# The pool engine gathers the second expert's rows ahead of all list scatters, and gets small copies that wait for the vector engine

## The chip, the cores and the metric

The kernel runs on one core of a Trainium2 chip. The metric is the device time in microseconds (us) of one execution; the number that counts is the median of several unprofiled runs. One further execution was taken with the hardware profiler, and all rows below are from it. PE is the matrix engine (PEld its weight loads), DVE the vector engine, ACT the scalar engine, POOL the engine that also issues indirect DMAs, SP the engine that issues most plain DMAs.

## The reference, cut to what matters

Three layers run one after the other: causal attention with a cumulative bias, a mixture of eight experts of which each token takes two, and a dense layer with the mish function. The change lies in the second:

```python
noisy_logits = x @ w_gate + np.log1p(np.exp(x @ w_noise)) * noise
top2 = np.argpartition(-noisy_logits, 2, axis=1)[:, :2]
top2_w = softmax over the two chosen logits
for e in range(8):
    for k in range(2):
        mask = top2[:, k] == e
        h = np.maximum(x[mask] @ w1[e], 0.0)
        out[mask] += top2_w[mask, k, None] * (h @ w2[e])
```

There are 1152 tokens of width 512; each expert has 1024 hidden units.

## The kernel before, in words

All of the work is issued in an order that is written out by hand, and each engine executes its own stream in that order. After attention the kernel routes: DVE picks the two experts of each token and works out a slot for each token in each expert's list, of 320 places (`CAP`). The lists of experts 0 and 1 are made at once on the chip (`quick_list`, line 737). The lists of all others are made in memory: 18 indirect DMAs from POOL (`scatter`, line 861) write token number and weight into the tensor `lst`, one DMA for 128 tokens and one of their two experts. Each later list comes back by three small loads from SP (`list_load`, line 767). With a list, three indirect DMAs from POOL fetch the rows of an expert's tokens into the tile `xg` (`xgather_chunk`, line 758).

An expert e is an up stage of eight steps f, some 1.8 us of PE each (line 897), and a down stage (line 962). After an up step ACT takes the positive part into the tile `HB[f]` (lines 899 and 900), and DVE writes what the rounding to the matrix format left out into the second part of the same tile (line 901). Then the step's hook `hup(f)` issues the side work of that step. In the down stage six hooks `hdn(c)` do the same; there the rows of expert e + 1 are also turned by PE (line 782) and split by ACT and DVE into `XH` and `XL` (lines 411 and 412). For experts 1 and 7 (`single`) the down stage goes through the eight `HB[f]` for the first block of rows before the second; for the others it goes through all three blocks for each f.

Side work is above all the preparing of weights for later: `convert` (line 254) has ACT copy a 128x512 weight to a rounded one (line 259) and either POOL or DVE subtract the two (line 260), which frees the raw tile for the next load from SP (lines 213 and 219). `narrow` (line 224) is DVE work alone, on integers, in three instructions for a weight of the third layer (lines 235, 237 and 239). Which engine subtracts stands in `MIXU` for the up steps (DVE for expert 0, POOL for all others) and in `MIXD` for the down stage (DVE and POOL by turns).

Before the change three scatters and the three gathers of expert 1 alternate ahead of the up stage of expert 0. Then each of its eight up hooks issues one scatter and a tiny POOL memset, and the down hooks call `scatter` twice each, until all 18 are out; that is in the seventh of these calls. A memset follows there in the calls in which POOL has no subtraction.

Of the kernel before, what the change touches and what calls it, by code (L numbers as in the profile page):

```python
# [9 lines left out]
F32 = mybir.dt.float32  # L10
# [18 lines left out]
CAP = 320  # L29
# [69 lines left out]
def f32(ap):  # L99
    return ap.bitcast(F32)  # L100
# [3 lines left out]
def kernel(ctx: ExitStack, tc: tile.TileContext, qT, kT, vv, ss, wg, nz, w1, w2,  # L104
# [55 lines left out]
    V, A, G_ = nc.vector, nc.scalar, nc.gpsimd  # L160
# [93 lines left out]
    def convert(sub, spare=0):  # L254

        for i, t in enumerate(tasks):
            if t["at"] == 5 and t["from"] <= at["now"] and t["step"] < at["step"] and len(places) > (spare if t["w"][0] >= 64 else 0):
                w = held[t["w"]] = places.pop(0)
                A.activation(w[:, 0], t["sv"], AF.Copy)  # L259
                sub(w[:, 1], t["sv"], f32(w[:, 0]))  # L260
                del tasks[i]
                if t["last"]:
                    at["out"] -= 1
                    fetch()
                return

    def work(subs, nv=0, spare=0):

        at["step"] += 1
        for i in range(max(len(subs), nv)):  # L270
            if i < len(subs):
                convert(subs[i], spare)
            if i < nv:
                narrow()
        start()
# [134 lines left out]
    def split(src, dsth, dstl):  # L410
        A.activation(dsth, src, AF.Copy)  # L411
        V.tensor_sub(dstl, src, f32(dsth))
# [99 lines left out]
    with tc.manual_schedule():  # L512
# [118 lines left out]
        for it in range(H + 2):  # L631
# [12 lines left out]
            for name in ORDERS[min(it, 3) if it < H - 1 else it - H + 5]:  # L644
                i = it + ("," not in name) + ("'" in name) - 1
# [6 lines left out]
    keep = ctx.enter_context(tc.tile_pool(name="keep", bufs=1, reuse_waits="tile"))  # L652
# [98 lines left out]
    XG, XH, XL = {}, {}, {}  # L751

    def xgather(e, idx):
        XG[e] = mp1.tile([128, 3, 512], F32, name="xg")
        for j in range(3):
            xgather_chunk(e, idx, j)

    def xgather_chunk(e, idx, j):
        m = BLK[j]
        nc.gpsimd.indirect_dma_start(  # L760
            out=XG[e][0:m, j], out_offset=None, in_=xd[:, :],
            in_offset=bass.IndirectOffsetOnAxis(ap=idx[0:m, j, 0:1], axis=0))
# [4 lines left out]
    def list_load(e, name="list"):  # L767
        idx = mp2.tile([128, 3, 2], I32, name=name, bufs=4 if name == "list" else None)
        r0 = first_row(e)
        nc.sync.dma_start(idx[:, 0:2], lst[r0:r0 + 256, :].rearrange("(j p) o -> p j o", p=128))  # L770
        for i in range(2):
            nc.sync.dma_start(idx[BLK[2] * i:BLK[2] * i + BLK[2], 2], lst[r0 + 256:r0 + CAP, :])
        return idx

    def xprep(e, c):
        if c == 0:
            XH[e] = mp1.tile([128, 4, CAP], F32R, name="xh")
            XL[e] = mp1.tile([128, 4, CAP], F32R, name="xl")
        xg = XG[e]
        t = next(psR)  # L780
        for j, m in enumerate(BLK):
            nc.tensor.transpose(t[:, 128 * j:128 * j + m], xg[0:m, j, 128 * c:128 * c + 128], identf[0:m, 0:m])  # L782
        split(t[:, :CAP], XH[e][:, c], XL[e][:, c])
# [77 lines left out]
    def scatter():  # L861


        if len(scat) < 2 * NT:
            t = len(scat) // 2
            ix = (idxa, idxb)[len(scat) % 2]
            st_ = nc.gpsimd.indirect_dma_start(
                out=lst[:, :], out_offset=bass.IndirectOffsetOnAxis(ap=ix[:, t:t + 1], axis=0),
                in_=tokw[:, t, len(scat) % 2], in_offset=None)
            for o in scat:  # L870
                tc.declare_no_dep(st_.ins, o.ins, reason="every slot is written once")
            scat.append(st_)

    for _ in range(2):
        convert(G_.tensor_sub)
    XG[1] = mp1.tile([128, 3, 512], F32, name="xg")
    for j in range(3):
        scatter()
        xgather_chunk(1, idx1, j)

    V.tensor_tensor(bcmp, inb[0:1, None, :].to_broadcast([1, NOV, E]),
# [7 lines left out]
    def up(e, hook):  # L889
        for f in range(8):  # L890
            ws = weight(8 * e + f // 2, f % 2)
            ps = next(psU)
            n = 0
            for c in range(4):
                wh, wl = ws[:, 0, 128 * c:128 * c + 128], ws[:, 1, 128 * c:128 * c + 128]
                for lhs, rhs in ((wh, XH[e][:, c]), (wh, XL[e][:, c]), (wl, XH[e][:, c])):
                    nc.tensor.matmul(ps[:, :CAP], lhs, rhs, start=n == 0, stop=n == 11)  # L897
                    n += 1
            nc.scalar.activation(HB[f][:, :CAP], ps[:, :CAP], AF.Relu)
            nc.scalar.activation(HB[f][:, 2 * CAP:], ps[:, 256:CAP], AF.Relu)  # L900
            V.scalar_tensor_tensor(HB[f][:, CAP:2 * CAP], ps[:, :CAP], 0.0, f32(HB[f][:, :CAP]),  # L901
                                   op0=OP.max, op1=OP.subtract)
            done_with(8 * e + f // 2, f % 2)
            hook(f)
# [4 lines left out]
    def first_gathers(k):  # L909

        if k == 0:
            FIRST["x"] = mp1.tile([128, GT, 512], F32, name="xg")
        for t in range(GT):
            nc.gpsimd.indirect_dma_start(
                out=FIRST["x"][:, t], out_offset=None, in_=yb[0:LA, :],
                in_offset=bass.IndirectOffsetOnAxis(ap=(idxa, idx0)[k][:, t:t + 1], axis=0),
                compute_op=(OP.bypass, OP.add)[k])

    def first_marks(idx):

        num = keep.tile([128, 3], F32, name="num")
        marks = mp1.tile([128, 4, CAP], F32R, name="xh").rearrange("p c n -> p (c n)")
        FIRST["mark"] = [marks[:, TG * j:TG * j + TG] for j in range(3)]
        for n, js in ((128, slice(0, 2)), (BLK[2], slice(2, 3))):
            V.tensor_scalar(num[0:n, js], idx[0:n, js, 0], 1.0, None, op0=OP.add)
        for j, m in enumerate(BLK):
            V.tensor_scalar(FIRST["mark"][j][0:m], iotac[0:m], num[0:m, j:j + 1], None, op0=OP.is_equal)
# [85 lines left out]
    def first_rows(j):  # L1013
        m = BLK[j]
        A.activation(Y0[0:m, j], Y0[0:m, j], AF.Copy, scale=f32(LISTS[0][0:m, j, 1:2]))
        nc.sync.dma_start(yb[first_row(0) + 128 * j:first_row(0) + 128 * j + m, :], Y0[0:m, j])
# [37 lines left out]
    HB = [mp3.tile([128, 2 * CAP + BLK[2]], F32R, name=f"h{f}") for f in range(8)]  # L1054
    Y0 = mp3.tile([128, 3, 512], F32, name="y0")
    LISTS = {}
    pad = keep.tile([128, 1], F32, name="pad")

    def expert(e):
        PV = {"p": G_.tensor_sub, "v": V.tensor_sub}  # L1060

        def hup(f):
            if e == E - 1:
                if f in (FG, FG + 1):
                    first_gathers(f - FG)
            if kept and f == 3:
                nc.sync.dma_start(*kept.pop())
            if e == 2 and f in (3, 5, 7):
                first_rows(f // 2 - 1)
            if e == 1 and f == 0:  # L1070
                LISTS[2] = list_load(2)
            if f == 6 and 0 < e < E - 2 and e != OVE:
                LISTS[e + 2] = list_load(e + 2)
            if (e, f) in ((1, 4), (2, 0)):
                LISTS[2 - e] = list_load(2 - e)
            if f == 2 and 0 < e < E - 1:
                xgather(e + 1, LISTS[e + 1])
            if e == 0:
                scatter()
                G_.memset(pad, 0.0)  # L1080
            work([PV[x] for x in MIXU[e][f % len(MIXU[e])]], NUP[e], SPAREU[e])
            at["now"] += 1

        def hdn(c):
            if e + 1 < E:
                for i in XPREP[c]:
                    xprep(e + 1, i)
            if e == OVE and c == OVV:
                n_blocks.append(nc.values_load(nblk[0:1, 0:1], min_val=0, max_val=NOV))
            if e == OVE and c == OVC:  # L1090
                at["stop"] = at["dma"]
            if e == E - 1 and c == 0:
                first_marks(LISTS[e])
            for x in MIXD[e] if e < E - 1 and (e != OVE or c < OVX) or e == E - 1 and c < 4 else ():
                if e == 0:
                    scatter()
                    if "p" not in x:
                        G_.memset(pad, 0.0)
                work([PV[y] for y in x], NDN[e], SPARED[e])
            at["now"] += 1  # L1100

        up(e, hup)
        down(e, hdn)

    for e in range(E):
# [136 lines left out]
    for n in range(N2 + LAG):  # L1242
        g, f = divmod(n, NF)
# [66 lines left out]
```

## Time and profile before

| | before |
|---|---|
| runs, median (lowest to highest) | 664.62 us (664.25 to 665.37), 3 runs |
| profiled execution | 669.99 us |
| its span, first to last instruction | 668.2 us |
| mean granted TensorE clock in the span | 0.97 |
| PE busy | 619.5 us |
| DVE busy | 498.1 us |
| POOL busy | 414.0 us |

The profiled execution took 5.37 us longer than the median of the others, and its span is 1.8 us shorter than its time. A busy share is a mean over stages that differ; what matters is where PE stands still, and for whom.

### The profile page before, as it was taken

How to read it: one execution, taken by the hardware profiler on the slowest of the kernel's cores; microseconds unless marked ns; L12 is line 12 of the kernel's file. 1: busy time of each engine (PE TensorE's matmuls, PEld its weight loads, DVE VectorE, ACT ScalarE, POOL GpSimd, SP SyncE). 2: the span in 40 equal slices, each digit the busy share in tenths (PEclk: the TensorE clock that was granted, in tenths of full speed). 3: DMA queues.
4: the chain of work that ended last, by engine and by line, in shares of the span. 5: the costliest groups of instructions: out<-in, count | busy, mean ns of one | idle time of the engine just before them, and what ended most of it. 6: DMA issues, size and time to landing. Idle time of an engine off the chain costs nothing.

```text
span 668.2 us, 10018 instructions
## 1 busy us (share of the span) xinstructions
PE 619.5 (93%) x3380; PEld 531.5 (80%) x3380; DVE 498.1 (75%) x814; ACT 379.9 (57%) x891; POOL 414.0 (62%) x382
## 2 busy tenths in 40 slices
PE   3799999999969899996999999997989999999997
PEld 2588888778849697976898979876768999899995
DVE  7598888658756858882858878958997868776863
ACT  3467767642436385743564647346657665766762
POOL 5868895435867575853765557617775857464652
PEclk9999999997979899997999999979999999999999
DMA  6847588442847787854664666804120113001001
GB/s 142 192 129 179 147 218 248 161 114 76 165 89 199 206 258 213 265 171 146 189 225 141 232 215 234 214 18 140 16 32 1 48 49 48 0 1 49 0 1 47
DMA packets 47605, 87.18 MB, mean 130 GB/s; under 512 B 18192, under 2 KB 25360, under 8 KB 47552
## 3 DMA queue, kind: packets, MB, share of 16 engines
q1 hardware_dynamic: 42128, 76.24, 39.7%
q0 software_dynamic: 4256, 9.98, 6.5%
q8 instruction: 27, 0.44, 0.3%
q10 hardware_dynamic: 1168, 0.29, 0.2%
q14 instruction: 26, 0.21, 0.1%
HBM read 70.68 MB, written 13.68 MB: 126 GB/s over the span
## 4 chain that ended last, share of the span: by engine, by line
PE 43%; DVE 7%; ACT 2%; issue 1%; ACTq 0%
PE bank L1220 12%; PE bank L1172 11%; PE bank L962 9%; PE bank L897 8%; DVE nn L1188 2%; DVE raw L237 1%; DVE rr L1201 1%; DVE ee L1208 1%; PE bank L782 1%; ACT ee L1185 1%; DVE raw L235 1%; PE bank L940 0%; DVE raw L239 0%; DVE ee L1184 0%; PE bank L932 0%
## 5 line engine op out<-in xcount | busy, mean ns | idle before, releaser
L260 POOL TENSOR_TENSOR w<-raw,w 128x512 fp32r<-128x512 f32 x107 | 144.4, 1383 | 106.1 <-ACT w L259 81.3
L962 PE MATMUL bank<-w,h 128*128 128x512 f32 (+1 forms) x512 | 130.5, 405 | 2.4 <-DVE h L901 2.4
L897 PE MATMUL bank<-xh,w 128*128 128x320 f32 x512 | 117.1, 314 | 6.3 <-SPq L1020 5.1
L962 PEld LDWEIGHTS bank<-w,h 128*128 128x128 f32 (+1 forms) x512 | 91.9, 185 | 28.1 <-DVE h L901 3.3
L259 ACT ACTIVATE w<-raw 128x512 fp32r<-128x512 f32 x148 | 90.5, 637 | 22.1 <-DVE raw L239 20.9
L1220 PE MATMUL bank<-w,gh 128*128 128x512 f32 x288 | 91.7, 400 | 5.4 <-ACT gh L1209 5.4
L1197 POOL TENSOR_TENSOR nn<-nn,rr 128x384 f32<-128x384 f32 x48 | 51.4, 1070 | 72.2 <-ACT nn L1196 63.0
L897 PEld LDWEIGHTS bank<-xh,w 128*128 128x128 f32 x512 | 87.7, 191 | 8.3 <-issue 5.5
L897 PE MATMUL bank<-xl,w 128*128 128x320 f32 x256 | 80.0, 312 | 0.0
L1172 PE MATMUL bank<-x2h,w 128*128 128x384 f32 x256 | 72.7, 349 | 0.9 <-ACT x2h L411 0.6
L1220 PEld LDWEIGHTS bank<-w,gh 128*128 128x128 f32 x288 | 54.1, 191 | 15.4 <-ACT gh L1209 6.7
L1220 PE MATMUL bank<-w,gl 128*128 128x512 f32 x144 | 58.4, 406 | 2.7 <-POOL gl L1210 2.7
L1188 DVE SCALAR_TENSOR_TENSOR nn<-ee 128x384 f32<-128x384 f32 x48 | 44.3, 924 | 22.1 <-ACT ee L1185 22.1
L1210 POOL TENSOR_TENSOR gl<-ee,gh 128x384 fp32r<-128x384 f32 x48 | 56.7, 1182 | 3.8 <-ACT gh L1209 2.2
L901 DVE SCALAR_TENSOR_TENSOR h<-bank,h 128x320 fp32r<-128x320 f32 x64 | 30.5, 485 | 35.3 <-ACT h L900 24.6
L1191 ACT ACTIVATE rr<-nn,two 128x384 f32<-128x384 f32 x48 | 29.6, 617 | 46.4 <-DVE nn L1188 46.4
L376 PE MATMUL s<-k,q 128*128 128x256 f32 (+3 forms) x96 | 38.2, 410 | 15.2 <-DVE k L544 9.5
L1172 PEld LDWEIGHTS bank<-x2h,w 128*128 128x128 f32 x256 | 48.9, 196 | 2.8 <-ACT x2h L411 1.1
L235 DVE TENSOR_SCALAR raw<-raw 128x512 int32<-128x512 int32 x32 | 50.0, 1563 | 0.0
L260 DVE TENSOR_TENSOR w<-raw,w 128x512 fp32r<-128x512 f32 x41 | 43.5, 1069 | 7.7 <-ACT w L259 6.2
L897 PEld LDWEIGHTS bank<-xl,w 128*128 128x128 f32 x256 | 48.9, 191 | 0.3
L439 ACT ACTIVATE pth<-pt 128x256 fp32r<-128x256 f32 (+4 forms) x88 | 32.7, 413 | 26.9 <-PE pt L422 26.6
(229 smaller groups left out, 1365.0 us busy)
## 6 DMA issues: line engine op xcount, KB each, us to landing
raw<-in SPq DMA_DIRECT2D x90, 512.0 KB
qd<-in SPq DMA_DIRECT2D x14, 320.0 KB
yb<-pth SPq DMA_DIRECT2D x1, 3584.0 KB
yb<-yr SPq DMA_DIRECT2D x14, 256.0 KB
rawa<-in SPq DMA_DIRECT2D x6, 512.0 KB
vr<-in SPq DMA_DIRECT2D x8, 320.0 KB
ke<-in SPq DMA_DIRECT2D x8, 288.0 KB
k<-k SPq DMA_DIRECT2D x7, 288.0 KB
```

The source lines that it names most:

```text
L235: V.tensor_scalar(lo32, lo32, 29, None, op0=OP.logical_shift_right)
L259: A.activation(w[:, 0], t["sv"], AF.Copy)
L260: sub(w[:, 1], t["sv"], f32(w[:, 0]))
L376: nc.tensor.matmul(o, a, b, start=first, stop=last)
L439: A.activation(x[1], x[0], AF.Copy)
L897: nc.tensor.matmul(ps[:, :CAP], lhs, rhs, start=n == 0, stop=n == 11)
L962: nc.tensor.matmul(ps[0:r], lhs, rhs, start=f + n == 0, stop=f == 7 and n == len(ms) - 1)
L1172: nc.tensor.matmul(ps[:, :TG], lhs, rhs, start=i == 0, stop=i == 11)
L1188: V.scalar_tensor_tensor(nn, ee, 2.0, ee, op0=OP.add, op1=OP.mult)
L1197: nc.gpsimd.tensor_mul(nn, nn, M[n][2])
L1210: nc.gpsimd.tensor_sub(gl, gg, f32(gh))
L1220: nc.tensor.matmul(qsD[i], lhs, rhs, start=f == 0 and m == 0, stop=f == NF - 1 and m == 2)
```

## The change

The three gathers of expert 1 no longer alternate with three scatters; a tiny memset stands ahead of each gather instead, and all 18 scatters go out from the hooks of expert 0. The tile `pad` that these memsets write is made earlier. A new function `in_step` is a POOL copy of one column of a tile into `pad`. It reads what DVE has just written, so POOL has to wait there for DVE. It is called in each of the 64 up hooks, on the part of `HB[f]` that DVE writes, and after each of the 28 splits of the next expert's rows. The memsets after the eight scatters of the up hooks go.

```diff
@@ -874,8 +874,9 @@
     XG[1] = mp1.tile([128, 3, 512], F32, name="xg")
+    pad = keep.tile([128, 1], F32, name="pad")
     for j in range(3):
-        scatter()
+        G_.memset(pad, 0.0)
         xgather_chunk(1, idx1, j)
@@ -1054,7 +1055,10 @@
     LISTS = {}
-    pad = keep.tile([128, 1], F32, name="pad")
+
+    def in_step(x):
+
+        G_.tensor_copy(pad, f32(x))
@@ -1075,9 +1079,9 @@
             if f == 2 and 0 < e < E - 1:
                 xgather(e + 1, LISTS[e + 1])
+            in_step(HB[f][:, CAP:CAP + 1])
             if e == 0:
                 scatter()
-                G_.memset(pad, 0.0)
             work([PV[x] for x in MIXU[e][f % len(MIXU[e])]], NUP[e], SPAREU[e])
@@ -1085,6 +1089,7 @@
                 for i in XPREP[c]:
                     xprep(e + 1, i)
+                    in_step(XL[e + 1][:, i, 0:1])
```

## Rows read from the trace of the kernel before

**Rows 1.** The page: busy time of each engine, then the clock in 40 slices.
```profile
PE 619.5 (93%) x3380; PEld 531.5 (80%) x3380; DVE 498.1 (75%) x814; ACT 379.9 (57%) x891; POOL 414.0 (62%) x382
...
PEclk9999999997979899997999999979999999999999
```

**Rows 2.** Timeline of PE: start, length, what, idle time before it.
```profile
191.41 0.99 PE L782 MATMUL bank<-identf,xg 128*128 128x128 f32 x3 [5.60 <-DVE xl L412]
...
219.68 0.58 PE L782 MATMUL bank<-identf,xg 128*128 128x128 f32 x3
...
224.44 1.86 PE L962 MATMUL bank<-w,h 128*128 128x512 f32 x5 [2.35 <-DVE h L901]
```

**Rows 3.** Stretches: length, PE, PEld, DVE, ACT, POOL busy, clock, DMA.
```profile
192.00:194.00 2.00, 2.00 (x6) 1.57 (x6) 1.97 (x3) 0.71 (x2) 1.84 (x2) 0.50 0.39 111
194.00:196.00 2.00, 2.00 (x7) 1.47 (x7) 1.93 (x4) 1.00 (x3) 1.79 (x4) 0.71 0.44 152
...
225.00:230.00 5.00, 4.97 (x16) 3.28 (x15) 4.35 (x8) 3.23 (x6) 2.09 (x2) 0.66 0.73 198
```

**Rows 4.** Timeline of ACT around the longest stop of PE.
```profile
180.30 0.44 ACT L899 ACTIVATE h<-bank 128x320 fp32r<-128x320 f32 x1 [3.81 <-remote]
...
190.39 0.44 ACT L411 ACTIVATE xh<-bank 128x320 fp32r<-128x320 f32 x1 [8.42 <-remote]
```

**Rows 5.** Timeline of DVE in the up stage of expert 1.
```profile
214.97 0.49 DVE L901 SCALAR_TENSOR_TENSOR h<-bank,h 128x320 fp32r<-128x320 f32 x1 [1.27 <-ACT h L899]
215.38 7.88 DVE L235 TENSOR_SCALAR raw<-raw 128x512 int32<-128x512 int32 x1
223.29 0.69 DVE L237 SCALAR_TENSOR_TENSOR raw<-ta,raw 128x512 int32<-128x512 int32 x1
223.90 0.48 DVE L901 SCALAR_TENSOR_TENSOR h<-bank,h 128x320 fp32r<-128x320 f32 x1
224.30 0.68 DVE L239 SCALAR_TENSOR_TENSOR raw<-raw 128x512 int32<-128x512 int32 x1
224.90 0.48 DVE L901 SCALAR_TENSOR_TENSOR h<-bank,h 128x320 fp32r<-128x320 f32 x1
```

**Rows 6.** Timeline of POOL in the same stage.
```profile
209.07 1.42 POOL L260 TENSOR_TENSOR w<-raw,w 128x512 fp32r<-128x512 f32 x1 [0.79 <-ACT w L259]
211.98 0.98 POOL L760 DMA_INDIRECT xg<-xd,list  x1 [1.49 <-DMA list<-lst]
213.26 0.96 POOL L760 DMA_INDIRECT xg<-xd,list  x1 [0.30 <-issue]
214.53 0.91 POOL L760 DMA_INDIRECT xg<-xd,list  x1 [0.30 <-issue]
215.46 7.51 POOL L260 TENSOR_TENSOR w<-raw,w 128x512 fp32r<-128x512 f32 x6
```

**Rows 7.** All instructions of line 235: shortest, median, longest ns.
```profile
L235 DVE TENSOR_SCALAR raw<-raw x32: 414/422/7884, 168.9 to 486.7; 128x512 int32<-128x512 int32 x32
```

**Rows 8.** Timeline of POOL and DVE in the up stage of expert 3.
```profile
280.23 7.53 POOL L260 TENSOR_TENSOR w<-raw,w 128x512 fp32r<-128x512 f32 x6
...
280.95 7.10 DVE L235 TENSOR_SCALAR raw<-raw 128x512 int32<-128x512 int32 x1
```

**Rows 9.** Timeline of POOL: gathers and scatters, first and last of 18.
```profile
167.04 1.02 POOL L867 DMA_INDIRECT lst<-tokw,idxa  x1 [1.38 <-DVE tokw L686]
168.37 1.49 POOL L760 DMA_INDIRECT xg<-xd,idx  x1 [0.30 <-issue]
...
174.29 0.91 POOL L760 DMA_INDIRECT xg<-xd,idx  x1 [0.31 <-issue]
175.51 1.01 POOL L867 DMA_INDIRECT lst<-tokw,idxb  x1 [0.30 <-issue]
176.52 0.11 POOL L1080 MEMSET pad<- 128x1 f32 x1
176.83 0.98 POOL L867 DMA_INDIRECT lst<-tokw,idxa  x1 [0.19 <-issue]
...
201.36 0.98 POOL L867 DMA_INDIRECT lst<-tokw,idxb  x1 [0.17 <-issue]
...
202.40 1.31 POOL L260 TENSOR_TENSOR w<-raw,w 128x512 fp32r<-128x512 f32 x1
203.64 0.27 POOL L1098 MEMSET pad<- 128x1 f32 x2
```

**Rows 10.** Timeline of SP: the loads of the list of expert 2.
```profile
207.55 0.38 SPq L770 DMA_DIRECT2D list<-lst  x1
```

**Rows 11.** Groups of POOL from 160 to 306 us: busy, mean ns, idle before.
```profile
L260 POOL TENSOR_TENSOR w<-raw,w 128x512 fp32r<-128x512 f32 x47 | 62.9, 1357 | 37.1 <-ACT w L259 33.5 <-PE bank L962 3.4
```

## The prediction

> **What bounds the kernel now.** I began with the page. PE is busy for 619.5 of 668.2 us and its clock dips in a few slices only [rows 1]; so the question is where PE stands still between routing and the end of the experts, the only stretch that the diff touches. The timeline of PE answers that. From 167 to 301 us, where the loop over overflow blocks begins, it has two stops of more than half a microsecond, and behind that loop none until the last expert is nearly done: 5.60 us ahead of a row turn at 191.41, and 2.35 us ahead of a down matmul at 224.44 [rows 2]. Each is followed by a stretch at the lower clock level (1.2 of 2.4 GHz), which the table of stretches prices: from 191.4 to 196 the mean clock of 0.50 and 0.71 loses about 0.3 + 1.0 + 0.6 = 1.9 us of work, and from 225 to 230 the mean of 0.66 loses 5 x 0.34 = 1.7 us [rows 3]. So 7.5 us hang on the first stop and 4.05 us on the second. That is all that better order of the side work can bring here; everything else between 167 and 301 us is PE at work.
>
> I then asked who caused each. The first stop runs through ACT: it waited 3.81 us for one up result and 8.42 us for the first turned rows, both marked as released by something that the trace doesn't record, while PE's matmuls that feed them had started long before [rows 4]. It falls into the burst of scatters [rows 9]. I can't tell from these rows what held ACT. But the profiled execution is 5.37 us over the median and the three runs lie within 1.12 us of each other, so I take it that most of this stop isn't in the timed runs. All sums below are therefore made against 664.62, that is 669.99 less 5.37, and the first stop counts there for at most 7.5 - 5.37 = 2.1 us.
>
> The second stop has a plain cause. In the up stage of expert 1 DVE's integer shift at line 235 began at 215.38 and took 7.88 us [rows 5]; the median of that instruction is 0.42 us [rows 7]. In exactly that time POOL ran six subtractions without a gap, 7.51 us from 215.46 [rows 6]. The shift ended when the sixth did, and the write of `HB[6]` that stood behind it came at 223.90, which is what PE waited for. POOL had this backlog since it had waited 1.49 us for the list and then issued three gathers. The same pair, a shift of 7.10 us under six subtractions of 7.53 us, stands in the stage of expert 3 [rows 8], with no stop of PE after it: there the down stage goes through all three blocks for each f, and needs the late tile later. So such a stall costs time only at expert 1 (and could at expert 7).
>
> **The change part by part.** *The copies.* 64 + 28 copies of one column are added. The trace has no such copy; the nearest row is the memset of one column, 0.11 us [rows 9]; the other bound is a whole subtraction, 1.36 us, but the work is one column of 512, so I take 0.12 us: 92 x 0.12 = 11 us of POOL over seven and a half expert stages. Eight memsets go and three come. POOL is idle for 37 us ahead of its subtractions between 160 and 306 us [rows 11], which covers its part of that. Without cover, while POOL is saturated from 167 to 209 us, about 14 copies are 1.7 us.
>
> *The wait in them.* Behind a waiting copy stand POOL's scatter or subtraction of that step, behind the subtraction the release of a raw tile and thus SP's next weight load. In the normal case the wait costs little: ACT's copy of the weight, which the subtraction needs anyway, is issued right after the same up step.
> What it buys is a limit to the backlog. With the rows of expert 1: the copies of steps 2 to 5 find their data written (the last of these writes starts at 214.97), so four subtractions still follow each other, 4 x (1.25 + 0.12) = 5.5 us from 215.46. The copy of step 6 then has to wait for DVE's write, which is behind the shift, so POOL's queue runs empty and the shift comes through at about 221.0, not at 222.9. `HB[6]` is then written at about 222.0, some 1.9 us sooner. The seventh write can still lose a part of it, since the next subtraction starts as soon as the sixth write is done and line 239 stands ahead of the seventh. Ends: nothing is gained if POOL's stream stays closed or the seventh write is as late as before, and 2.35 + 1.7 = 4.05 us if PE never stops. I take half, 2.0 us. At the experts after that the stall shrinks also (from six to about three subtractions at expert 3), for nothing, as PE doesn't wait there.
>
> The row says that a shift waits for a whole train of subtractions. The Trainium skill (SBUF — State Buffer, Who interferes with whom) has a rule by which DVE and POOL share a port pair as an exclusive lock that is held for a whole instruction, and the other fully blocks. Taken word for word that is a wait for one subtraction, about 1.3 us, and then a limit on the train would bring nothing (the first rival's time, 664.6). The trace differs, with 7.88 us against six subtractions, so I weigh the train.
>
> *The gathers first.* They wait for neither the slot work nor a scatter, so they go out about as soon as POOL's two subtractions are done, near 165.7 instead of from 168.37 on [rows 9], and the third ends near 170 instead of at 175.2. PE took the rows without a stop before, so this is worth nothing; it hides in the up stage of expert 0.
>
> *The scatters.* Three move from ahead of expert 0 into its down stage; the last one goes from the seventh to the tenth call there. One scatter with its memset or copy is about 1.3 us [rows 9]. Where POOL is the bound, three fewer stand ahead: 201.36 - 3.9 + 3 x 1.3 + one subtraction of 1.3 = 202.7. Where the pace of the stage is, it is behind the memset of the ninth call, at about 203.9, and the two scatters that then still queue make it 205.2 at the latest. So the last scatter is 1.3 to 3.8 us later. SP's list load, at 207.55 [rows 10], needs it landed; the nearest row for a small DMA's way is the list itself, 207.55 to 211.98, 4.4 us. I take the low end, with the load about as late as before, as it stands behind a weight load on SP's queue anyway.
>
> Sum: 664.62 - 2.0 = 662.6 us.
>
> **The rivals.** *No change.* POOL runs so far behind DVE in expert 1 that the copies never wait before the damage is done, or the gap doesn't let DVE in. For it: four of six steps are satisfied by the rows. Against it: the sixth surely isn't. Time 664.6, within 0.2% (1.33 us, about what a measurement of this kernel can tell from no change).
>
> *Slower: the list of expert 2 comes late.* At the upper end the last scatter ends at 206.2 and lands at 210.6, and the load goes out 3.0 us later. POOL stands at the gathers, which end at 218.4 instead of 215.44. PE turns these rows at 219.68 [rows 2], and with 4.4 us for landing there was no slack. PE would stop for up to 3.0 us and lose another 1.7 at the lower clock: 4.7 at most, 2.5 in the middle, 667.1 us. It decides from a delay of the list of about 1 us. Against it: late gathers let the shift through before the subtractions begin, which gives some back.
>
> *The first stop is in the timed runs as well, and goes,* since the scatters of the down stage are now held to DVE's pace. For it: it falls into the burst. Against it: the 5.37 us. Up to 7.5 more, so about 655 us.
>
> **How the numbers follow.** The likeliest, 0.36, is the shortened train with 1.4 to 4.05 us gained (660.6 to 663.2; I predict 662.6). No change has 0.33. The late list, with any other loss through POOL's waits, has 0.22, mostly from 666 to 669. The first stop's removal has 0.09. Faster is 0.36 + 0.09 = 0.45, same 0.33, slower 0.22. The range from 658.0 to 667.5 leaves out most of the last case and the tail of the slower one, together under 0.2.
>
> **What would show it.** Right: in the up stage of expert 1 no more than four subtractions of POOL in a train, a shift of line 235 under 6 us, POOL waiting for line 901 in the copies, and PE's stop of 2.35 us shorter; the later long shifts down to about 4 us. Gathers of expert 1 ahead of 170. Wrong: trains of six as before; the list load after 209 and PE waiting for turned rows; new stops of PE behind late weights, which would mean that POOL's waits reach SP's loads. If the timed runs drop by over 6 us, the first stop was real.

## The result and the profile after

| | before | after |
|---|---|---|
| median of 15 runs each, on one chip | 665.90 us | 671.53 us |
| ratio, 95% interval | | 1.0065 (1.0038 to 1.0092) |
| profiled execution | 669.99 us | 669.26 us |
| its span | 668.2 us | 667.5 us |

The change made the kernel slower, by 4.3 us going by the ratio, while the two medians lie 5.6 us apart; a second comparison on another chip gave 1.0033 (1.0002 to 1.0065). One run of before, of 758.42 us, is a slow one and isn't in the ratio. The profiled execution of after lies 2.3 us under the median of its runs (666.37 to 674.40), so its rows are read for places, not for the sum.

The page's busy times, to be held against [rows 1]: PE is busy for 3 us less with the same instructions, DVE for 6 us less, and POOL for 21 us more.
```profile
PE 616.3 (92%) x3380; PEld 529.9 (79%) x3380; DVE 492.4 (74%) x814; ACT 380.7 (57%) x891; POOL 435.3 (65%) x469
```

The timeline of PE after, as in [rows 2], its stops of more than a microsecond without the one of some 5 us at the loop over overflow blocks, which every execution has:
```profile
208.56 0.42 PE L898 MATMUL bank<-xh,w 128*128 128x320 f32 x1 [3.76 <-DVE h L902]
223.20 2.50 PE L963 MATMUL bank<-w,h 128*128 128x512 f32 x5 [2.51 <-DVE h L902]
...
414.54 0.42 PE L898 MATMUL bank<-xh,w 128*128 128x320 f32 x1 [1.28 <-DVE h L902]
438.58 0.44 PE L941 MATMUL bank<-xh,xl 64*128 64x384 f32 x1 [1.77 <-ACT xl L997]
```
The first stop of before, 5.60 us ahead of a row turn, is gone; a new one of 3.76 us stands in the up stage of expert 1; the second stop is still there, 2.51 us where it was 2.35; and there are two in the last expert. Two stretches at a low clock follow the stops in expert 1 (columns as in [rows 3]):
```profile
208.00:213.00 5.00, 4.43 (x20) 4.44 (x21) 2.00 (x5) 1.63 (x4) 0.28 (x1) 0.66 0.29 74
...
223.00:228.00 5.00, 4.80 (x15) 3.53 (x16) 4.38 (x8) 2.79 (x6) 4.72 (x6) 0.68 0.52 119
```
So one stop and its low clock went and another came, and the stop that the copies were to shorten stayed. The rows of POOL, answering to [rows 6, 9], show why the second part is not simply that the copies did nothing:
```profile
166.32 1.04 POOL L760 DMA_INDIRECT xg<-xd,idx  x1
...
168.92 1.37 POOL L760 DMA_INDIRECT xg<-xd,idx  x1 [0.19 <-DVE h L902]
...
202.08 0.97 POOL L867 DMA_INDIRECT lst<-tokw,idxb  x1 [0.19 <-PE bank L898]
...
212.72 1.00 POOL L760 DMA_INDIRECT xg<-xd,list  x1 [5.62 <-DMA list<-lst]
...
216.21 0.19 POOL L1061 COPY pad<-h 128x1 f32<-128x1 f32 x1
216.36 1.29 POOL L260 TENSOR_TENSOR w<-raw,w 128x512 fp32r<-128x512 f32 x1
...
220.48 1.25 POOL L260 TENSOR_TENSOR w<-raw,w 128x512 fp32r<-128x512 f32 x1
223.28 0.51 POOL L1061 COPY pad<-h 128x1 f32<-128x1 f32 x1 [1.55 <-DVE h L902]
```
The train is four subtractions, with a copy ahead of each, and the next copy waits 1.55 us for DVE: as forecast. But it begins at 216.36, after POOL has stood for 5.62 us for the list of expert 2. DVE, against [rows 5]:
```profile
202.65 4.73 DVE L235 TENSOR_SCALAR raw<-raw 128x512 int32<-128x512 int32 x1
...
216.57 0.49 DVE L902 SCALAR_TENSOR_TENSOR h<-bank,h 128x320 fp32r<-128x320 f32 x1 [5.79 <-ACT h L901]
216.97 5.04 DVE L235 TENSOR_SCALAR raw<-raw 128x512 int32<-128x512 int32 x1
222.05 0.69 DVE L237 SCALAR_TENSOR_TENSOR raw<-ta,raw 128x512 int32<-128x512 int32 x1
222.66 0.48 DVE L902 SCALAR_TENSOR_TENSOR h<-bank,h 128x320 fp32r<-128x320 f32 x1
```
The shift takes 5.04 us and not 7.88, yet PE waits for the write behind it as long as before, since DVE had itself waited 5.79 us for ACT. The new stop of 3.76 us has the shape that the prediction gave to the old one: from 203.10 POOL worked off three subtractions behind the last scatter, the two copies between them (at 204.35 and 205.71) found their data written and didn't wait, the shift at 202.65 took 4.73 us, and the write behind it came at 208.03. SP and ACT say what ACT waited for:
```profile
209.76 0.38 SPq L770 DMA_DIRECT2D list<-lst  x1
210.19 1.15 SPq L772 DMA_DIRECT2D list<-lst  x2
211.43 0.53 SPq L219 DMA_DIRECT2D raw<-in  x1
```
```profile
215.43 0.66 ACT L249 ACTIVATE ta<-raw 128x512 f32<-128x512 f32 x1 [4.66 <-DMA raw<-in]
```
The list load, against [rows 10], is out at 209.76. Expert 1 starts at 194.7 here, so that is 15.0 us later (in the profile of before expert 1 itself was 7 us late, by the first stop; in a second one of the same kernel, without that stop, the load comes 10.9 us after the start). SP stood there for 4.9 us until the last scatter had landed, at 209.70; in the profile of before it doesn't wait for a scatter at this load. SP issues its loads in the order of the program, so the weight load behind it goes at 211.43; ACT's copy of that weight (line 249), and behind it the positive part of the next up step, wait 4.66 us for it.

The copies themselves, all instructions of the line (shortest, median, longest ns, first and last start):
```profile
L1061 POOL COPY pad<-h x64: 175/188/785, 170.3 to 426.0; 128x1 f32<-128x1 f32 x64
L1061 POOL COPY pad<-xl x28: 175/223/672, 182.9 to 398.0; 128x1 f32<-128x1 f32 x28
```
None takes 0.12 us. The groups of POOL over the whole execution (columns as in [rows 11]) add their busy time and their waits:
```profile
L1061 POOL COPY pad<-h 128x1 f32<-128x1 f32 x64 | 18.1, 284 | 28.0 <-DVE h L902 27.9
L1061 POOL COPY pad<-xl 128x1 f32<-128x1 f32 x28 | 10.3, 369 | 18.8 <-DVE xl L412 18.8
```

### The profile page after: what moved, and what is told of

It is laid out like the page before. It is cut to its first block, busy times and chain, and to the rows that moved or that the text cites. A ratio compares the mean times of both kernels' runs of the same rounds, so it can differ in the third digit from the quotient of the medians.

```text
span 667.5 us, 10198 instructions
## 1 busy us (share of the span) xinstructions
PE 616.3 (92%) x3380; PEld 529.9 (79%) x3380; DVE 492.4 (74%) x814; ACT 380.7 (57%) x891; POOL 435.3 (65%) x469
## 3 DMA queue, kind: packets, MB, share of 16 engines
q1 hardware_dynamic: 42128, 76.24, 40.9%
## 4 chain that ended last, share of the span: by engine, by line
PE 40%; DVE 8%; ACT 3%; issue 2%; DMA 1%; POOL 1%; ACTq 0%; POOLq 0%; DVEq 0%
PE bank L1225 12%; PE bank L1177 12%; PE bank L898 7%; PE bank L963 7%; DVE nn L1193 2%; DVE raw L237 1%; DVE xl L998 1%; DMA yb<-yr 1%; DVE rr L1206 1%; PE bank L782 1%; DVE ee L1213 1%; ACT ee L1190 1%; DVE raw L235 1%; ACT rr L1196 0%; DVE raw L239 0%
## 5 line engine op out<-in xcount | busy, mean ns | idle before, releaser
L963 PE MATMUL bank<-w,h 128*128 128x512 f32 (+1 forms) x512 | 128.7, 402 | 2.5 <-DVE h L902 2.5
L898 PEld LDWEIGHTS bank<-xh,w 128*128 128x128 f32 x512 | 88.3, 192 | 13.5 <-DVE h L902 7.7
L902 DVE SCALAR_TENSOR_TENSOR h<-bank,h 128x320 fp32r<-128x320 f32 x64 | 30.5, 485 | 37.2 <-ACT h L901 37.0
L260 DVE TENSOR_TENSOR w<-raw,w 128x512 fp32r<-128x512 f32 x41 | 45.8, 1126 | 9.4 <-ACT w L259 9.1
L398 ACT ACTIVATE p<-s,nm 128x128 f32<-128x128 f32 (+4 forms) x72 | 39.3, 556 | 14.8 <-PE s L376 6.3
L439 ACT ACTIVATE pth<-pt 128x256 fp32r<-128x256 f32 (+4 forms) x88 | 32.7, 414 | 26.3 <-PE pt L422 26.1
```

Of the source, the lines that this page charges most:

```text
L398: A.activation(o, src, AF.Exp, bias=NM[h][:, i:i + 1], scale=-1.0, accum_out=SM[h][:, i:i + 1])
L439: A.activation(x[1], x[0], AF.Copy)
L963: nc.tensor.matmul(ps[0:r], lhs, rhs, start=f + n == 0, stop=f == 7 and n == len(ms) - 1)
```

## The experiments

Fifteen kernels were run, each 12 times, the ratio taken to runs of the kernel before on the same chip. In the expectations four theories have letters. **A**: the moved scatters make the list of expert 2 late, and the weight load behind it on SP holds ACT. **B**: the waits in the copies cost a little everywhere. **C**: the copies cost time in the last expert. **D**: the early gathers themselves cost, as they meet other loads.

The profile of each gives two stage times, from the first up matmul of an expert to that of another, or to the first matmul of the dense layer (after: expert 0 starts at 162.6, expert 2 at 236.9, difference 74.3; expert 7 at 400.5, the layer at 441.3, 40.8):

```
kernel                 ratio (95% interval)         experts 0+1      expert 7
before                 -                            39.5+36.9 = 76.4   39.1
before_again           0.9998 (0.9975 to 1.0021)    32.1+43.5 = 75.6   39.3
order_only             1.0029 (1.0004 to 1.0053)    32.1+43.6 = 75.7   39.4
gathers_then_scatters  1.0029 (1.0001 to 1.0057)    38.8+39.6 = 78.4   39.0
after_nowait           1.0057 (1.0039 to 1.0075)    32.1+43.3 = 75.4   39.2
catch_up_plain         1.0019 (0.9993 to 1.0045)    36.2+40.6 = 76.8   39.0
steps_0_only           1.0011 (0.9980 to 1.0041)    32.3+44.1 = 76.4   38.9
steps_7_only           1.0037 (1.0006 to 1.0068)    32.2+41.5 = 73.7   40.6
steps_late             1.0051 (1.0018 to 1.0085)    39.4+39.4 = 78.8   42.0
steps_only             1.0042 (1.0020 to 1.0064)    32.1+40.6 = 72.7   40.8
steps_early            0.9963 (0.9936 to 0.9990)    32.1+41.4 = 73.5   39.2
steps_to_6             0.9978 (0.9949 to 1.0007)    32.7+40.5 = 73.2   38.8
steps_to_6_again       0.9968 (0.9944 to 0.9991)    32.1+40.5 = 72.6   38.8
order_steps_early      1.0007 (0.9981 to 1.0034)    31.8+42.2 = 74.0   38.8
catch_up_to_6          0.9954 (0.9929 to 0.9979)    32.1+40.6 = 72.7   39.2
after                  1.0065 (1.0038 to 1.0092)    32.1+42.2 = 74.3   40.8
after_again            1.0033 (1.0002 to 1.0065)    32.1+44.8 = 76.9   40.7
```

### The two halves of the change

**order_only** has the gathers first and the scatters moved, without copies:
```diff
     for j in range(3):
-        scatter()
+        G_.memset(pad, 0.0)
         xgather_chunk(1, idx1, j)
```


> The kernel before with the new order alone: the three gathers of expert 1 first, all scatters from the hooks, none of the copies that wait for the vector engine. Theory A (the late list): the last scatter comes some 1 to 4 us later, SP's list load for expert 2 with it, and the weight load queued behind the list load then holds ACT; the loss sits here, so this is slower than before by 3 to 6 us. Theory B (the waiting copies): the order is harmless, within 1.5 us of before.

**steps_only** has the copies, in the old order:
```diff
+            in_step(HB[f][:, CAP:CAP + 1])
             if e == 0:
                 scatter()
-                G_.memset(pad, 0.0)
...
                     xprep(e + 1, i)
+                    in_step(XL[e + 1][:, i, 0:1])
```


> The changed kernel with the scatters put back among the gathers, so that only the 92 waiting copies are new. Theory A: within 1.5 us of before, and SP's list load for expert 2 not later than the end of the eighth up step of expert 0 would allow. Theory B: the copies, at 0.2 to 0.8 us each and with POOL held at DVE, cost 3 to 6 us by themselves.

**after_nowait** is the changed kernel with memsets in place of the copies, so that nothing waits:
```diff
     def in_step(x):
-        G_.tensor_copy(pad, f32(x))
+        G_.memset(pad, 0.0)
```


> The changed kernel with each waiting copy replaced by a memset of the same column, which waits for nothing: same order, same number of POOL instructions. Theory A: as slow as the changed kernel, +4 to +6 us. Theory B: the wait was the cost, so within 1.5 us of before. Trains of six subtractions should be back in either case.

**before_again** is the kernel before without an edit.

> The kernel before itself, to see how far two kernels that are the same come apart, and for a second profile of it. If the stop of 5.60 us ahead of 191 us belongs to the one profiled execution, it is missing here, and the profiled time is near 665 us; the up stage of expert 1 then begins some 7 us sooner, while POOL still works off the scatters. If it belongs to the kernel, it is here again.

Measured: 1.0029, 1.0042, 1.0057 and, for no edit, 0.9998. Each half alone costs time. By size neither theory holds: the order alone costs 1.9 us, where A had 3 to 6 and B less than 1.5; the copies alone cost 2.8 us, where A had less than 1.5 and B 3 to 6. In before_again the first stop is missing, but the execution took 668.54 us and not some 665. Taking the waits away doesn't help, so B isn't the whole loss. It also takes the gain of the copies away, if they have one; this set can't tell.

### Where the copies gain and lose

**after_again** is the changed kernel once more.

> The changed kernel once more, beside the parts of it and on the same chip, with a second profile. Expected again 0.4 to 0.9% over before. The first profile of it gives expert 1 (from its first up matmul to that of expert 2) 42.2 us, expert 4 32.9 us and expert 7 up to the third layer 40.9 us. If the loss sits in the waits of expert 1 (theory A, the late list), a typical execution has over 43 us there; if it sits in expert 7 (theory C, below), the 40.9 us is repeated.

**steps_early** and **steps_late** are steps_only with the copies in experts 0 to 3 and 4 to 7 alone:
```diff
-            in_step(HB[f][:, CAP:CAP + 1])
+            if e < 4:
+                in_step(HB[f][:, CAP:CAP + 1])
...
-                    in_step(XL[e + 1][:, i, 0:1])
+                    if e < 4:
+                        in_step(XL[e + 1][:, i, 0:1])
```
(for the late half e > 3; there the memset behind each scatter stays.)

> The order of before, with the waiting copies in experts 0 to 3 only. Theory A or any theory that puts the cost of the copies at the burst of scatters and the list of expert 2: +1.5 to +3 us, as in the run with all copies. Theory C, that the copies cost where DVE and POOL work on the third layer's weights at expert 7: no loss here, and a gain of up to 2 us if the shorter trains at expert 1 count.

> The order of before, with the waiting copies in experts 4 to 7 only. Theory C: expert 4 shorter by 0.7 us, as the long shift there shrinks, expert 7 longer by 1.6 us, together about +1 us. Theory A: no change, within 0.5 us, or a gain.

**gathers_then_scatters** has the three gathers, then three scatters each with a memset, and from there on the hooks of before:
```diff
     for j in range(3):
-        scatter()
+        G_.memset(pad, 0.0)
         xgather_chunk(1, idx1, j)
+    for j in range(3):
+        scatter()
+        G_.memset(pad, 0.0)
```


> The order of before but for the alternation: three gathers first, then three scatters with a memset each, then the hooks as before; no waiting copies. The last scatter stays in the seventh call of the down stage. Theory A: no loss, within 1 us of before, and less than the order alone. If the early gathers themselves cost (theory D: they and the weight loads meet), it is as slow as the order alone, about +2 us.

Measured: 1.0033; 0.9963, faster; 1.0051; 1.0029. The same edit gains in the first experts and loses in the last ones. gathers_then_scatters is evidence against A as the whole price of the order: its last scatter is not moved, and it is slower as well, at the edge of its interval.

### Which expert, and what the order costs with the copies

**steps_to_6** has the condition e < 7, **steps_7_only** e == 7 (with the memsets of before), **steps_0_only** e == 0, all in the old order. **order_steps_early** is the changed kernel with e < 4.

> The kernel before, with the copies in experts 0 to 6 (and on the split rows of experts 1 to 7), the order of gathers and scatters as before. Theory C (in the last expert the copies start POOL's subtractions together with DVE's integer work on the third layer's weights, for some 1.6 to 2.7 us): without the eight copies of expert 7 the loss goes and the gains of experts 0, 1 and 4 stay, about 3 + 0.8 us, ratio 0.994; the profile's last expert lasts 39 to 39.4 us and not 40.8. Theory B (every waiting copy costs a little): worse than the copies in experts 0 to 3 alone (0.9963), about 0.999.

> The kernel before with eight copies alone, those of the up steps of expert 7. Theory C: slower by 1.6 to 2.7 us, ratio 1.0024 to 1.004, with the last expert at 40.7 to 42 us in the profile and a stop of PE over 1 us near the end of its up stage. If eight copies in expert 7 are not the cause: ratio 1.000, last expert 39 to 39.4 us.

> The kernel before, with the copies of expert 0 alone (8 on up results, 4 on the split rows of expert 1). If what copies gain early is the stop of 5 to 7 us of PE at the row turns of expert 0, and that stop is in most runs: its down stage ends at 32.1 us and not at 39, ratio about 0.995 to 0.998, as the following expert gives a part back (its train of six subtractions is not cut). If the gain is the shorter train in expert 1, as the prediction had it: ratio 1.000.

> The changed kernel (gathers ahead of all scatters) with the copies of experts 0 to 3 alone. Against the same copies in the old order (0.9963) it tells what the moved scatters cost once the copies are there. Theory A (last scatter and so the list of expert 2 come later, and the weight load behind the list on SP's queue holds ACT): 2 to 3 us worse, ratio 0.9995 to 1.001, with the list load some 15 us behind the start of expert 1 and not 13.5. If the order is worth nothing, as the prediction had it: 0.996 again.

Measured: 0.9978, 1.0037, 1.0011, 1.0007. Eight copies in the last expert cost 0.37%, some 2.5 us, and without them the rest is no loss: C, although C had 0.994 for the rest and 0.9978 was measured. In the profiles the last expert lasts 40.6 to 42.0 us in all five executions that have these copies and 38.8 to 39.4 us in all twelve that don't. The copies of expert 0 alone gain nothing, although the first stop is absent from that profile: expert 1 gives it back, 44.1 us. And the same copies that gave 0.9963 in the old order give 1.0007 in the new one, as A expects; the two intervals just overlap.

How eight copies lose 2 us is seen by putting after beside steps_to_6. DVE in the up stage of the last expert, then POOL there, after:
```profile
411.10 0.42 DVE L235 TENSOR_SCALAR raw<-raw 128x512 int32<-128x512 int32 x1
411.55 1.81 DVE L237 SCALAR_TENSOR_TENSOR raw<-ta,raw 128x512 int32<-128x512 int32 x1
413.40 0.69 DVE L239 SCALAR_TENSOR_TENSOR raw<-raw 128x512 int32<-128x512 int32 x1
414.00 0.48 DVE L902 SCALAR_TENSOR_TENSOR h<-bank,h 128x320 fp32r<-128x320 f32 x1
...
423.75 6.10 DVE L998 TENSOR_TENSOR xl<-yr,xl 128x512 fp32r<-128x512 f32 x1 [0.70 <-ACT xl L997]
```
```profile
411.31 0.24 POOL L1061 COPY pad<-h 128x1 f32<-128x1 f32 x1 [1.81 <-DVE h L902]
411.51 1.29 POOL L260 TENSOR_TENSOR w<-raw,w 128x512 fp32r<-128x512 f32 x1
...
423.23 0.79 POOL L1061 COPY pad<-h 128x1 f32<-128x1 f32 x1
423.38 1.92 POOL L260 TENSOR_TENSOR w<-raw,w 128x512 fp32r<-128x512 f32 x1
```
The same places in steps_to_6, where expert 7 starts 1.3 us sooner (399.2 and 400.5), DVE, then POOL,
```profile
410.68 0.69 DVE L239 SCALAR_TENSOR_TENSOR raw<-raw 128x512 int32<-128x512 int32 x1
411.29 0.48 DVE L902 SCALAR_TENSOR_TENSOR h<-bank,h 128x320 fp32r<-128x320 f32 x1
...
421.23 5.02 DVE L998 TENSOR_TENSOR xl<-yr,xl 128x512 fp32r<-128x512 f32 x1 [0.70 <-ACT xl L997]
```
```profile
408.06 1.57 POOL L260 TENSOR_TENSOR w<-raw,w 128x512 fp32r<-128x512 f32 x1 [0.86 <-ACT w L259]
...
420.00 5.70 POOL L260 TENSOR_TENSOR w<-raw,w 128x512 fp32r<-128x512 f32 x4
```
and PE behind them:
```profile
435.07 0.44 PE L941 MATMUL bank<-xh,xl 64*128 64x384 f32 x1 [0.97 <-ACT xl L997]
```
In this stage DVE has a shift and the two instructions at 237 and 239 between almost any two writes of `HB`. A copy that waits for such a write releases POOL's subtraction in the same moment as the next three integer instructions, and line 237 takes 1.81 us in place of 0.69. The write at 414.00 comes 13.5 us after the expert's start; in steps_to_6 it is 12.1. Later the train lies on DVE's line 998 for 6.10 us and not 5.02, and PE waits 1.77 us ahead of line 941 where steps_to_6 has 0.97. These are 1.4 + 0.8 = 2.2 us, against 40.8 - 38.8 = 2.0. The pair of stops goes with the copies: all five executions that have them show 1.1 to 1.3 us in this up stage and 1.6 to 2.1 us ahead of line 941; the twelve others show none over 0.8 us in the up stage and 0.8 to 1.0 us ahead of line 941.

That the second stop does go in expert 1 when the list is in time is seen in steps_to_6 as well. PE, a stretch, POOL, and ACT:
```profile
222.12 1.74 PE L963 MATMUL bank<-w,h 128*128 128x512 f32 x5 [0.46 <-DVE h L902]
```
```profile
222.00:227.00 5.00, 4.83 (x20) 3.49 (x21) 4.90 (x10) 3.36 (x6) 4.80 (x6) 1.00 0.42 103
```
```profile
211.62 1.00 POOL L760 DMA_INDIRECT xg<-xd,list  x1 [2.26 <-PE bank L898]
...
219.39 1.26 POOL L260 TENSOR_TENSOR w<-raw,w 128x512 fp32r<-128x512 f32 x1
```
```profile
213.81 0.66 ACT L249 ACTIVATE ta<-raw 128x512 f32<-128x512 f32 x1 [1.24 <-DMA raw<-in]
```
0.46 us and full clock, against 2.51 us and 0.68 in after. ACT waits 1.24 us for the weight, not 4.66. In order_steps_early, where only the order is different, the late chain is back (SP, ACT, PE):
```profile
214.46 0.38 SPq L770 DMA_DIRECT2D list<-lst  x1
```
```profile
220.18 0.67 ACT L249 ACTIVATE ta<-raw 128x512 f32<-128x512 f32 x1 [5.42 <-DMA raw<-in]
```
```profile
227.52 1.74 PE L963 MATMUL bank<-w,h 128*128 128x512 f32 x5 [2.74 <-DVE h L902]
```
Its expert 1 starts at 198.0, so the list load is 16.5 us behind that start (15.0 in after, 12.9 in steps_to_6).

All seventeen profiled executions agree with this. At the list load SP waits for the last scatter for 4.9 to 7.0 us in the five with moved scatters, and for 3.4 us at most in the twelve others. PE's stop ahead of the down stage of expert 1 is 1.4 to 4.8 us in the nine without copies in expert 1, 1.7 to 2.7 us in the three with the copies and a late list, and 1.3 us at most in the five with the copies and the list in time.

### The scatters brought forward

**catch_up_to_6** keeps the early gathers, has the copies in experts 0 to 6, and lets the first three up steps of expert 0 issue the three moved scatters:
```diff
             if e == 0:
                 scatter()
+                if f < 3:
+                    G_.memset(pad, 0.0)
+                    scatter()
```
**catch_up_plain** does the same without copies (a memset behind each scatter), and **steps_to_6_again** is the old order with the copies of experts 0 to 6, as a measure on the same chip.

> The changed kernel without the eight copies of expert 7, and with the three moved scatters issued earlier: each of the first three up steps of expert 0 issues two scatters, with a memset between them, so that the last of the 18 is out as early as in the kernel before, while the gathers stay ahead of all scatters. If the order costs time because the last scatter and with it the list of expert 2 come later: the loss goes, ratio 0.996 to 0.998 as with the same copies in the old order, list load some 13 us after the start of expert 1, and a stop of PE at the first down matmul of expert 1 of about 1 us or less. If the early gathers themselves cost the time: ratio 1.000 to 1.001.

> The kernel before with the three gathers ahead of all scatters, the three moved scatters issued in the first three up steps of expert 0, and no copies. If the late last scatter is what the order costs: 1.000. If the early gathers cost: 1.003, as when the scatters go to the end (1.0029) or right behind the gathers (1.0029).

> The old order with the copies of experts 0 to 6 once more, as the measure for the first of these kernels, on the same chip: 0.996 to 0.998. If it is not below 1 here, no version of the copies is shown to be faster than the kernel before.

Measured: 0.9954, 1.0019 and 0.9968. With the copies, the loss of the order goes when the last scatter is out in time, so A holds and D doesn't: the gathers are as early as in after. The rows of catch_up_to_6 (POOL, SP, a stretch); expert 1 starts at 195.6 and the list load follows 13.3 us later:
```profile
201.68 1.28 POOL L867 DMA_INDIRECT lst<-tokw,idxb  x1 [0.16 <-issue]
...
212.90 1.01 POOL L760 DMA_INDIRECT xg<-xd,list  x1 [1.81 <-DMA list<-lst]
```
```profile
208.87 0.38 SPq L770 DMA_DIRECT2D list<-lst  x1
```
```profile
223.00:228.00 5.00, 4.79 (x21) 3.25 (x20) 4.98 (x9) 3.36 (x6) 4.50 (x6) 1.00 0.44 108
```
PE has no stop over 0.4 us at the end of the up stage there, and the clock stays full. Without copies the result, 1.0019, lies between the two expectations and settles nothing. catch_up_to_6 is the version that beats both kernels: 0.9954 (0.9929 to 0.9979), some 3 us under the kernel before.

## Why the prediction was wrong

**What bounds the kernel: the reading of the first stop failed.** The prediction took most of the 5.60 us for an accident of one execution, because the profiled time was 5.37 us above a median of three runs that lay within 1.12 us. Three runs say little: on two other chips 35 runs of the kernel before lay between 661.51 and 670.66 us and 29 between 664.81 and 672.59 us, and on the first chip the median of fifteen was 665.90 and not 664.62. The stop is real. Of the six profiled kernels without copies in expert 0 whose scatters are out early, four spend 36.2 to 39.5 us in expert 0 (two lose it in one stop, as here in steps_late, PE and then ACT, the others in pieces):
```profile
191.28 0.98 PE L782 MATMUL bank<-identf,xg 128*128 128x128 f32 x3 [4.97 <-DVE xl L412]
```
```profile
190.27 0.44 ACT L411 ACTIVATE xh<-bank 128x320 fp32r<-128x320 f32 x1 [8.39 <-remote]
```
The thirteen other executions, two of those six among them, spend 31.8 to 32.7 us. But the rival that priced its removal at 7.5 us was wrong too: where expert 0 is short, expert 1 is long. Its up stage has 2.7 to 6.5 us of stops over 0.8 us in all thirteen executions with a short expert 0, whatever the kernel, and 1.5 us at most in the four with a long one. The pairs of the table without copies in the first experts and in the old order sum to 76.4 and 78.8 with a long expert 0, and to 75.6 and 73.7 with a short one. So most of a wait that goes in one stage came back in the next; four executions don't tell how much of it is won.

**The shortened train: right, with its size.** Trains of four, a copy waiting for line 902, a shift under 6 us: all three are in the profile after. The gain of 2.0 us that was forecast for it is what the copies bring once nothing else is spoilt: 0.9963, 0.9978 and 0.9968, that is 1.5 to 2.5 us. Where expert 0 is short, expert 1 lasts 40.5 to 41.4 us with the copies and the list in time, and 41.5 to 44.1 us without copies. The shift at line 235 was only one form of the stall: in before_again line 237 took 8.31 us under the six subtractions and PE stopped for 3.30 us, in steps_late line 239 took 7.90 us and PE stopped for 3.39 us. What the prediction missed is that after doesn't show the gain, because the train of expert 1 hangs on the list. Read as a wait for one subtraction, as the prediction read it, the Trainium skill's rule (SBUF — State Buffer, Who interferes with whom) of a lock held for a whole instruction had this gain at nothing. The traces don't bear that reading out: a shift took 5.04 us under four subtractions, and cutting the train gained time.

**The copies' price: mis-sized, and the first step that failed, in one expert.** 92 copies took 18.1 + 10.3 = 28.4 us, not 11, and POOL stood 46.7 us more in their waits; but with experts 0 to 6 alone they cost nothing that shows. The failed step is that the cover was taken to be the same in all experts. The prediction noted that a stall *could* cost time in expert 7 and left it at that; there POOL's subtraction, tied to DVE's write, lands on DVE's integer work: 1.0037 by itself.

**The scatters: the second step that failed.** The forecast had the last scatter 1.3 to 3.8 us later and then took the low end with the list load "about as late as before", hidden behind a weight load on SP's queue. It isn't hidden: SP waited there for the scatter itself (4.9 us in after), which landed 6.7 us after its end, where the forecast took 4.4 us. Counted from the start of expert 1 the load went out 15.0 to 17.0 us later in after, after_again and order_steps_early, against 12.9 to 13.6 us with copies and the scatters in time. The rival *the list of expert 2 comes late* named this, with 2.5 us in the middle and 4.7 at most; measured, it is 1.0007 against 0.9963, and 0.9954 against 1.0007 (each ratio to the kernel before on its own chip), about 3 us, each difference known to some 2.5 us. The profiles give 0.8 to 4.3 us: expert 1 lasts 42.2, 44.8 and 42.2 us in those three, and 40.5 to 41.4 us in the five with the list in time. Its path was only half right: it had PE waiting for turned rows. That wait is 1.25 us in after_again and absent from after; the larger part goes by SP's queue, where the weight load stands behind the list, to ACT. Late weights were among the prediction's signs of being wrong, but by POOL's waits, not by the order of SP's queue.

**The gathers first: worth nothing, as forecast.** They are out at 166.32 to 170.29, and catch_up_to_6 and steps_to_6_again differ by less than their intervals.

For after the parts add up in the timed runs: copies in experts 0 to 6 about -0.3%, the eight of expert 7 +0.37%, the order +0.4 to 0.5%, together +0.5 to 0.6%, against 0.65 and 0.33 measured. Both failed steps together are shown by catch_up_to_6, which mends both and gains; their shares are not. The same sum gives steps_only about +0.1%, and 0.42% (0.20 to 0.64) was measured, so the copies alone already turned the sign, and against steps_only the moved scatters add nothing that is clear of noise. The profiles don't explain this: from the start of expert 0 to the layer steps_only and after_nowait take 277.3 and 279.0 us, the two executions of before 279.9 and 279.4. What is later is the start of expert 0, at 164.7 and 165.4 us against 162.2 and 161.1, and that lateness arises before 41 us, ahead of every edited instruction. Whether it is the chance spread of the last section or goes with the kernel is not shown.

**Open** stay also: what ACT waits for in the first stop; what the order costs without copies, where three kernels gave 1.0019 to 1.0029 and neither A nor D is excluded; why the version with memsets was as slow as 1.0057; and why the stage times of the two profiled executions alone, 74.3 + 40.8 and 76.4 + 39.1, show nearly no loss.

## What to carry to other kernels

Before a train of side work is cut, look up what stands at its head: here it began when a list landed, so three scatters that moved behind others cost about as much as the shorter train gained. On a queue that issues in order, as SP's does here, a late small load is priced by the big load behind it, and by the engine that needs that one. An edit that ties one engine to another's step should be tried stage by stage: the same copies gained 2 us in the first experts and lost 2.5 us in the last, and a median of the whole shows only the difference. One profile of a kernel like this one is not enough to name a stop: the same code took 39.5 + 36.9 us for its first two experts in one execution and 32.1 + 43.5 us in the next.

## What the runs showed of the hardware

A POOL copy of one column took 0.175 us at the least and up to 0.785 us, while a memset of the same tile took 0.11. The thirty longest, from 0.325 us on, all overlap an instruction of DVE, but so do many of the shortest, so what makes a copy long is not shown.

Executions of identical code differ in their first 41 us. One stretch of before_again and of after_again, which are the same up to there:
```profile
28.00:36.00 8.00, 6.59 (x41) 4.94 (x39) 6.99 (x12) 5.75 (x21) 7.59 (x13) 1.00 0.68 160
```
```profile
28.00:36.00 8.00, 6.76 (x26) 4.64 (x24) 5.76 (x9) 4.48 (x17) 7.75 (x12) 1.00 0.84 183
```
In about the same busy time PE ran 41 matmuls in one and 26 in the other, though the granted clock reads 1.00 in both; expert 0 starts at 161.1 us in the first and 164.8 us in the second. The seventeen profiled executions fall into two groups: the hundredth matmul starts at 37.2 to 38.4 us in nine and at 39.4 to 41.1 us in eight, and the changed kernel is in both (38.0 in after, 40.9 in after_again). Expert 0 starts between 161.1 and 166.2 us. That spread is as large as the effect studied.
